# The second MoE's weight pieces: decoded in the y stages alone instead of in y and x2

## The chip, the cores and the metric

The kernel runs on one core of a Trainium2 chip. The metric is device time in microseconds of one execution, and the time before is the median of three runs, 1390.62 us (1390.1 to 1392.14). One execution was also taken by the hardware profiler; it took 1393.72 us, and its span from the first to the last instruction is 1391.8 us. The engines are named as the profile names them: PE (TensorE), DVE (VectorE), ACT (ScalarE), POOL (GpSimd), and SP, the engine whose queue issues nearly all transfers.

## What is computed

An attention block, a first MoE and a second MoE in a row; a token's vector has 512 numbers, and there are 8 x 576 = 4608 tokens.

```python
p_packed = sm_attn(p, k, v)              # 32 packed queries per head
out = sm_attn(q, p_packed, p_packed)     # softmax over 32
h = np.maximum(np.maximum(x @ w1, x @ w2), x @ w3)     # 512 -> 768
x2 = h @ w_out                                         # 768 -> 512
h = x2 @ w_in                                          # 512 -> 2048
g = P(h) / (Q(h) + 1e-06)                # polynomials of h, element by element
y = g @ w_out2                           # 2048 -> 512
```

The weights come in as 64-bit floats. The kernel decodes them itself, from two 32-bit words each, into a high and a low part in fp32, and each large product is made of three: high by high, high by low, low by high (`mm3`, lines 60 to 63).

## The kernel before, in words

The first 593 us of the span handle the batches in four pairs (`bp`, 0 to 3); the second MoE follows over blocks of 512 tokens. Each pair has two stages.

*y stage* (`y_stage`, line 447). For each of six column blocks f and both batches b2, three products (w1, w2, w3) go into PSUM tiles `psy`, of which there are two. ACT copies the first into `hm` (L459), and DVE takes the maximum with the second and third (L461). ACT then makes the high part `hh`, and POOL (DVE in pair 0) the low part `hl`. After each of the 36 products, counted t = 0 to 35, `between` (line 540) does small steps of other work: the m stage for the next f (`m_stage`, line 303, PE's line 313, at t mod 6 of 2 and 4), a step of the next pair's attention (the list PACK), and, at the t in `y_steps`, one step of the decode of the second MoE's weights.

*x2 stage* (`x2_stage`, line 468). Eight products (m of 4, b2 of 2) with `w_out`, each of 36 matmuls into `psy`; ACT or DVE copies it out (L477) and it is stored to DRAM. Between them stand the second half of the next pair's attention (the list SECOND: a softmax on POOL, DVE and ACT, lines 267 to 297, and the first two m stages of the next pair) and, for the indices in `windows`, more steps of the decode. Pair 3 has neither.

*The decode* (`decode`, line 68, called through `Feed`, line 103). There are 32 pieces of 128 x 512 weights. Each is loaded (512 KB, L100, three buffers `w_raw`), taken apart by DVE (L76, L80), converted by ACT (L81, L82), put together by DVE (L85, L87, L92) and POOL (L95) into a `wt` tile, and stored to DRAM (512 KB, L235), from where the second MoE loads it. `step()` is `finish()` of one piece and then `start()` of the next: L76, L80, L81 and L82 belong to the start, the others to the finish, and the load of a later piece follows it. 33 steps decode 32 pieces.

*The wt tiles.* There are four (line 184). The m stage's own weights use them too: they were decoded in pair 0 and are loaded again from DRAM in later pairs (`again`, line 213, L216), four m stages ahead.

*The order.* The code is not run in the order in which it is written. With `schedule_with_timeline_sim` (line 731) a scheduler simulates the engines when the kernel is built, and fills each engine's queue; of the instructions that are ready in its simulation it takes the one that was written first, and it hands out tile buffers in the same way. On the chip each queue is then run strictly in that order.

Of the kernel before, what the change touches and what calls it, by code (L numbers as in the profile page):

```python
# [33 lines left out]
def attn_moe_moe2_kernel(  # L34
# [16 lines left out]
    def split(hi, lo, src, hi_eng="act", lo_eng="dve"):  # L51

        if hi_eng == "act":
            act.copy(hi, src)  # L54
        else:
            nc.vector.tensor_copy(hi, src)
        e = dve if lo_eng == "dve" else pool
        e.tensor_tensor(out=lo, in0=src, in1=hi.bitcast(F32), op=ALU.subtract)  # L58
# [165 lines left out]
    def w2_pieces():  # L224

        for i in range(32):
            box = []

            def tiles(box=box):
                box.append(wt_tile())  # L230
                hi, lo = (box[0][:, x] for x in range(2))
                return (hi.bitcast(I32) if wide else hi.bitcast(F32R)), lo.bitcast(F32R)

            def keep(box=box, i=i):
                nc.sync.dma_start(w2_scr[:, :, 512 * i : 512 * i + 512], box[0])  # L235

            yield tiles, w_2[i], keep, False

    def load_w2(tiles, o, n):

        for x in range(2):
            nc.sync.dma_start(tiles[:, x].bitcast(F32), w2_scr[:, x, 512 * o : 512 * (o + n)])
# [56 lines left out]
    def m_tiles(f):  # L299

        return [mp[f % 2].tile([128, 2, 2, 384], F32R, name=f"m{x}") for x in "hl"]

    def m_stage(bp, g, mt):

        ps = ps_t.tile([128, 2, 512], F32, name="pst")
        wt, n = next_wt()
        for b2 in range(2):
            for h in range(4):  # L310
                i, j = divmod(h, 2)
                l, c = slice(64 * j, 64 * j + 64), 32 * (h ^ b2)
                pe.matmul(ps[c : c + 32, b2, :384], lhsT=ppk[l, bp % 2, 2 * g + b2, 32 * h : 32 * h + 32],  # L313
                          rhs=wt[l, 384 * i : 384 * i + 384], start=True, stop=True)
        again(n)
        split(*(t[:, :, g, :] for t in mt), ps[:, :, :384])
# [130 lines left out]
    def y_stage(b2, f, m, a2, between, lo_eng):  # L447
        hm = hx.tile([128, 2, 288], F32, name="hm")
        mh, ml = m
        for w in range(3):  # L450
            ps = ps_y.tile([128, 2, 512], F32, name="psy")
            for half in range(2):
                for g in range(2):
                    ah, al = a2[g]
                    c = slice(288 * half, 288 * half + 288)
                    mm3(ps[:, half, :288], mh[:, g, 128 * w : 128 * w + 128], ml[:, g, 128 * w : 128 * w + 128],
                        ah[:, c], al[:, c], g == 0, g == 1)
            if w == 0:
              act.copy(hm, ps[:, :, :288])  # L459
            else:  # L460
              dve.tensor_tensor(out=hm, in0=ps[:, :, :288], in1=hm, op=ALU.max)  # L461
            between()
        hh = hp_pool.tile([128, S], F32R, name=f"hh{b2}{f}")
        hl = hp_pool.tile([128, S], F32R, name=f"hl{b2}{f}")
        split(hh, hl, hm.rearrange("p a b -> p (a b)"), lo_eng=lo_eng)
        return hh, hl

    def x2_stage(b, m, hs):
        ps = ps_y.tile([128, 2, 512], F32, name="psy")
        for half in range(2):  # L470
            c = slice(288 * half, 288 * half + 288)
            for f in range(6):
                hh, hl = hs[f]
                mm3(ps[:, half, :288], wo_h[:, m, 128 * f : 128 * f + 128], wo_l[:, m, 128 * f : 128 * f + 128],
                    hh[:, c], hl[:, c], f == 0, f == 5)
        xs = hx.tile([128, 2, 288], F32, name="hm")
        (act.copy if m < 3 else dve.tensor_copy)(xs, ps[:, :, :288])  # L477
        nc.sync.dma_start(x2_scr[:, m, S * b : S * b + S], xs.rearrange("p a b -> p (a b)"))

    def wi_at(f):  # L480

        if f < 1:
            return wi_0
        return wi_b[:, :, f - 1]
# [26 lines left out]
    pool.memset(cln[:, 1:2], -LN64)  # L511
    feed2 = None

    y_steps = {1: range(1, 36, 4), 2: range(1, 36, 4), 3: range(1, 32, 4)}
    windows = (), (0, 2, 4, 6), (1, 3, 5)
    for bp in range(NBP):
        turn = itertools.count()
        if bp == 1:
            feed2 = Feed(wp, w2_pieces(), NRAW, NRAW)
        if bp == NBP - 1:  # L520

            nc.sync.dma_start(av, a_in.partition_broadcast(128))
            nc.sync.dma_start(bv, b_in.partition_broadcast(128))
            dve.tensor_scalar(out=babs, in0=bv, scalar1=-1.0, scalar2=None, op0=ALU.mult)
            dve.tensor_tensor(out=babs, in0=babs, in1=bv, op=ALU.max)
        now = ahead
        a2, mt = ahead.a2, ahead.mt
        hs = [[None] * 6, [None] * 6]
        if bp + 1 < NBP:
            ahead = Ahead(bp + 1)  # L530
            for x in "P L0 W0 L1 W1".split():
                ahead.do(x)
            pack = ahead.steps(PACK)
        else:
            pack = iter(())
        for f in range(6):
            if f < 5:
                nmt = m_tiles(f + 1)

            def between(bp=bp, f=f, now=now):  # L540
                t = next(turn)
                if now.soft:
                    now.do("g")
                if f < 5 and t % 6 in (2, 4):
                    m_stage(bp, t % 6 // 2 - 1, nmt)
                if t >= 2:
                    next(pack, None)
                if bp == 0:
                    if t % 3 < 2 and t < 32:
                        feed.half_step()  # L550
                elif t in y_steps[bp]:
                    feed2.step()

            if bp == NBP - 1 and f == 2:
                load_w2(wi_at(0), 0, 1)
            for b2 in range(2):
                hs[b2][f] = y_stage(b2, f, [t[:, b2] for t in mt], a2[b2], between,
                                    "dve" if bp == 0 or (b2, f) == (1, 5) else "pool")
            mt = nmt
        if bp + 1 < NBP:  # L560
            assert not list(pack)
            gen = ahead.steps(SECOND)
            for m in range(4):
                for b2 in range(2):
                    x2_stage(2 * bp + b2, m, hs[b2])
                    next(gen, None)
                    if bp == 0:
                        feed.half_step()
                    if 2 * m + b2 in windows[bp]:
                        feed2.step()  # L570
            if bp == 0:
                assert not feed.raw and not feed.half
            next(gen, None)
            assert not ahead.soft
        else:
            assert not feed2.raw and not feed2.half
            rstack.close()
            NQA = 1
            wr = ctx.enter_context(tc.tile_pool(name="wr", bufs=1, side="right"))
            xpa = ctx.enter_context(tc.tile_pool(name="xpa", bufs=1, side="right"))  # L580
            wi_b = wr.tile([128, 2, 15, 512], F32R, name="wi_b")
            wq_a = wr.tile([128, 2, NQA, DM], F32R, name="wq_a")

            def wq_at(f):
                return wq_a[:, :, f] if f < NQA else wq_b[:, :, f - NQA]

            def load_x(blk, xp):
                xh = xp.tile([128, 4, 512], F32R, name="xh")
                xl = xp.tile([128, 4, 512], F32R, name="xl")
                for kc in range(4):  # L590
                    xr = xp.tile([128, 512], F32, name="xr", bufs=1)
                    nc.sync.dma_start(xr, x2_scr[:, kc, 512 * blk : 512 * blk + 512])
                    split(xh[:, kc, :], xl[:, kc, :], xr, lo_eng="pool" if blk > 1 else "dve")
                return xh, xl

            loads = [(wi_at(f), f) for f in range(1, 16)] + [(wq_at(f), 16 + f) for f in range(NQA)]
            per = -(-len(loads) // 8)
            for b2 in range(2):
                for m in range(4):
                    for _ in range(min(per, len(loads))):  # L600
                        tiles, o = loads.pop(0)
                        load_w2(tiles, o, 1)
                    if (b2, m) == (0, 2):
                        xc = load_x(0, xpa)
                    x2_stage(2 * bp + b2, m, hs[b2])
# [129 lines left out]
```

## Time and profile before

| | |
|---|---|
| median of three runs | 1390.62 us |
| the profiled execution | 1393.72 us |
| its span | 1391.8 us |
| PE busy in the span | 1313.8 us (94%) |
| DVE, ACT, POOL busy | 76%, 58%, 17% |
| pair 0, y and x2 | 54.0 to 171.0 and to 215.8 us |
| pair 1, y and x2 | to 297.4 and to 350.4 us |
| pair 2, y and x2 | to 432.7 and to 487.5 us |
| pair 3, y and x2 | to 554.5 and to 593.0 us |

The busy shares are means over stages with different limits, so the stages are looked at one by one. The bounds of a stage are read from the names on PE's matmuls: psy<-a2h,mh is a product of y, psy<-hh,wo_h one of x2. A busy PE is not a PE at full speed, so the granted clock stands beside the busy time.

### The profile page before, as it was taken

What the parts mean: (1) busy time and instruction counts of PE and PEld (TensorE: products, weight loads), DVE (VectorE), ACT (ScalarE), POOL (GpSimd) and SP (SyncE); (2) the same over time, 40 slices, a digit from 0 to 9 for tenths busy, and PEclk for the clock granted to TensorE, in tenths of its full rate; (3) what the DMA queues carried; (4) which work ended last, traced back from release to release, by engine and by line L of the source; (5) the groups of instructions that cost most, each with busy time, mean ns of one, the idle gap of its engine ahead of it and who ended that gap; (6) DMA issues with size and microseconds to landing.
All of it is one profiled execution on the core that took longest, in us unless ns stands there. A gap on an engine that the chain in (4) does not pass through costs nothing.

```text
span 1391.8 us, 21572 instructions
## 1 busy us (share of the span) xinstructions
PE 1313.8 (94%) x8496; PEld 1091.5 (78%) x8496; DVE 1051.1 (76%) x1630; ACT 802.2 (58%) x1337; POOL 242.7 (17%) x230
## 2 busy tenths in 40 slices
PE   4479899998999899999999999999999999999998
PEld 1267788878878789978888888888888888888886
DVE  5877845767677765178888988888888888888887
ACT  3444523543443333176766867768677686776765
POOL 3542242425333533000100101001010010100000
PEclk9589899999999999999999999999999999999999
DMA  9945544677464721970100101001001010010000
GB/s 307 308 138 167 158 144 145 213 230 245 155 209 156 237 93 55 325 278 1 47 14 1 61 1 38 23 0 62 0 25 37 0 54 0 16 38 1 31 0 31
DMA packets 51557, 140.86 MB, mean 101 GB/s; under 512 B 5632, under 2 KB 5632, under 8 KB 50688
## 3 DMA queue, kind: packets, MB, share of 16 engines
q1 hardware_dynamic: 51168, 138.96, 30.0%
q8 instruction: 67, 1.10, 0.3%
q10 hardware_dynamic: 288, 0.52, 0.1%
q14 instruction: 34, 0.28, 0.1%
HBM read 99.09 MB, written 40.37 MB: 100 GB/s over the span
## 4 chain that ended last, share of the span: by engine, by line
PE 81%; DVE 5%; DMA 4%; ACT 2%; issue 1%; POOL 1%; SPq 0%; ACTq 0%; POOLq 0%; DVEq 0%
PE po L61 10%; PE po L62 9%; PE po L63 9%; PE psh L62 9%; PE psh L61 9%; PE psh L63 9%; PE psy L61 8%; PE psy L62 7%; PE psy L63 7%; PE pst L313 2%; DMA wi_b<-w_scr 1%; DMA w_raw<-in_w_dram 1%; DMA x_scr<-hm 1%; PE pst L378 1%; DVE wt L87 1%
## 5 line engine op out<-in xcount | busy, mean ns | idle before, releaser
L61 PE MATMUL po<-wq_b,gh 128*128 128x512 f32 x540 | 212.3, 393 | 0.8 <-ACT gh L54 0.8
L62 PE MATMUL po<-wq_b,gh 128*128 128x512 f32 x540 | 211.3, 391 | 0.0
L62 PE MATMUL psh<-xl,wi_b 128*128 128x512 f32 x540 | 211.0, 391 | 0.0
L63 PE MATMUL psh<-xh,wi_b 128*128 128x512 f32 x540 | 210.6, 390 | 0.0
L61 PE MATMUL psh<-xh,wi_b 128*128 128x512 f32 x540 | 210.6, 390 | 0.0
L634 ACT ACTIVATE hb<-psh,babs 128x512 f32<-128x512 f32 (+1 forms) x145 | 100.2, 691 | 188.8 <-PE psh L63 188.8
L61 PE MATMUL psy<-a2h,mh 128*128 128x288 f32 x576 | 181.6, 316 | 17.1 <-DVE hm L461 8.1
L63 PE MATMUL po<-wq_b,gl 128*128 128x512 f32 x540 | 181.7, 391 | 0.0
L637 DVE SCALAR_TENSOR_TENSOR hb<-h,babs,hb 128x512 f32<-128x512 f32 (+1 forms) x145 | 108.2, 746 | 97.1 <-ACT h L635 97.0
L62 PE MATMUL psy<-a2l,mh 128*128 128x288 f32 x576 | 172.7, 300 | 4.4 <-POOL a2l L58 4.4
L63 PE MATMUL psy<-a2h,ml 128*128 128x288 f32 x576 | 172.0, 299 | 0.0
L58 POOL TENSOR_TENSOR xl<-xr,xh 128x512 fp32r<-128x512 f32 x28 | 36.6, 1306 | 633.5 <-ACT xh L54 633.5
L61 PEld LDWEIGHTS psy<-a2h,mh 128*128 128x128 f32 x576 | 110.3, 192 | 44.4 <-issue 12.9
L61 PE MATMUL psy<-hh,wo_h 128*128 128x288 f32 x384 | 117.2, 305 | 12.1 <-ACT hm L477 11.7
L63 PEld LDWEIGHTS po<-wq_b,gl 128*128 128x128 f32 x540 | 101.3, 188 | 24.0
L461 DVE TENSOR_TENSOR hm<-psy,hm 128x576 f32<-128x576 f32 x96 | 72.4, 754 | 63.2 <-PE psy L63 60.3
L61 PEld LDWEIGHTS po<-wq_b,gh 128*128 128x128 f32 x540 | 101.4, 188 | 22.9 <-ACT gh L54 1.2
L62 PEld LDWEIGHTS po<-wq_b,gh 128*128 128x128 f32 x540 | 101.4, 188 | 22.4
L61 PEld LDWEIGHTS psh<-xh,wi_b 128*128 128x128 f32 x540 | 101.4, 188 | 22.1
L62 PEld LDWEIGHTS psh<-xl,wi_b 128*128 128x128 f32 x540 | 101.4, 188 | 21.7
L63 PEld LDWEIGHTS psh<-xh,wi_b 128*128 128x128 f32 x540 | 101.4, 188 | 21.7
L62 PE MATMUL psy<-hl,wo_h 128*128 128x288 f32 x384 | 115.5, 301 | 0.0
(104 smaller groups left out, 2816.0 us busy)
## 6 DMA issues: line engine op xcount, KB each, us to landing
w_raw<-in_w_dram SPq DMA_DIRECT2D x32, 512.0 KB, 4.7
w_scr<-wt SPq DMA_DIRECT2D x32, 512.0 KB, 3.3
wt<-w_scr SPq DMA_DIRECT2D x36, 384.0 KB, 4.0
kt<-in_k_dram SPq DMA_DIRECT2D x16, 576.0 KB, 6.2
vraw<-in_v_dram SPq DMA_DIRECT2D x16, 576.0 KB, 6.5
w_raw<-in_w_dram SPq DMA_DIRECT2D x12, 768.0 KB, 12.0
kt<-in_q_dram SPq DMA_DIRECT2D x16, 576.0 KB, 6.2
x_scr<-hm SPq DMA_DIRECT2D x32, 288.0 KB, 3.3
```

The source lines that it names most:

```text
L58: e.tensor_tensor(out=lo, in0=src, in1=hi.bitcast(F32), op=ALU.subtract)
L61: pe.matmul(out_ap, lhsT=lh, rhs=rh, start=first, stop=False)
L62: pe.matmul(out_ap, lhsT=lh, rhs=rl, start=False, stop=False)
L63: pe.matmul(out_ap, lhsT=ll, rhs=rh, start=False, stop=last)
L87: dve.scalar_tensor_tensor(out=hib, in0=hw, scalar=-0x80000000, in1=t, op0=ALU.bitwise_and, op1=ALU.bitwise_or)
L313: pe.matmul(ps[c : c + 32, b2, :384], lhsT=ppk[l, bp % 2, 2 * g + b2, 32 * h : 32 * h + 32], rhs=wt[l, 384 * i : 384 * i + 384], start=Tru ...
L378: pe.matmul(pv[32 * h : 32 * h + 32, :64], lhsT=at[:, 3 * i + cp, o : o + 32], rhs=vt[:, h, c, :], start=c == 0, stop=c == VC - 1)
L461: dve.tensor_tensor(out=hm, in0=ps[:, :, :288], in1=hm, op=ALU.max)
L634: act.activation(hb, h, AF.Abs, scale=babs[:, 0:1])
L637: dve.scalar_tensor_tensor(out=hb, in0=h2, scalar=babs[:, 1:2], in1=hb, op0=ALU.mult, op1=ALU.add)
```

## The change

The steps of the decode of the second MoE's pieces are taken out of x2, and there are more of them in y: after every third product in pairs 1 and 2 (12 each instead of 9), and after every fourth, with one more at the end, in pair 3 (9 instead of 8). The steps in x2, 4 in pair 1 and 3 in pair 2, go. The number of steps stays 33.

```diff
-    y_steps = {1: range(1, 36, 4), 2: range(1, 36, 4), 3: range(1, 32, 4)}
-    windows = (), (0, 2, 4, 6), (1, 3, 5)
+    y_steps = {1: range(1, 36, 3), 2: range(1, 36, 3), 3: range(1, 36, 4)}
...
                     next(gen, None)
                     if bp == 0:
                         feed.half_step()
-                    if 2 * m + b2 in windows[bp]:
-                        feed2.step()
```

## Rows read from the trace of the kernel before

**Rows 1.** Stages: start:end, length, then busy us (records) PE, PEld, DVE, ACT, POOL, clock.

```profile
54.00:171.00 117.00, 93.16 (x900) 74.02 (x908) 95.04 (x136) 56.74 (x92) 38.98 (x36) 0.85 0.53 172
171.00:215.80 44.80, 44.41 (x401) 40.03 (x386) 19.54 (x34) 11.74 (x18) 14.92 (x12) 1.00 0.38 126
215.80:297.40 81.60, 79.31 (x869) 66.68 (x876) 52.49 (x91) 37.24 (x69) 29.79 (x34) 1.00 0.60 188
297.40:350.40 53.00, 47.59 (x401) 43.14 (x388) 39.19 (x66) 19.60 (x31) 24.77 (x18) 0.94 0.74 253
...
432.70:487.50 54.80, 48.48 (x433) 43.08 (x433) 43.22 (x71) 21.39 (x33) 25.89 (x19) 0.94 0.71 235
487.50:554.50 67.00, 65.41 (x530) 58.96 (x530) 38.29 (x53) 24.58 (x38) 22.31 (x16) 1.00 0.21 72
```

**Rows 2.** What TensorE waited for, x2 of pairs 1 and 2: us, times, longest.

```profile
PE psy L61 <- ACT hm L477: 5.4, 3, 2.4
...
PE psy L61 <- ACT hm L477: 6.3, 2, 5.3
```

**Rows 3.** Timeline before one wait: start, duration us, instruction, [idle before, releaser].

```profile
310.00 1.54 POOL L283 TENSOR_TENSOR e<-e,mx 128x576 f32<-128x576 f32 x1 [1.94 <-DVE mx L282]
...
310.44 1.38 DVE L80 TENSOR_SCALAR dec_r<-w_raw 128x512 int32<-128x512 int32 x1
...
311.85 0.63 ACT L82 ACTIVATE dec_r<-dec_r 128x512 f32<-128x512 int32 x1 [1.95 <-DVE dec_r L80]
...
312.96 0.62 ACT L477 COPY hm<-psy 128x576 f32<-128x576 f32 x1
```

**Rows 4.** Two stretches behind waits, columns as above.

```profile
313.60:317.20 3.60, 3.57 (x15) 3.57 (x16) 3.60 (x9) 0.63 (x1) 2.17 (x2) 0.53 0.48 185
466.20:473.00 6.80, 6.80 (x35) 6.80 (x36) 6.50 (x12) 2.71 (x4) 5.28 (x4) 0.66 0.77 259
```

**Rows 5.** Line 87 in y1, its x2, pair 2's x2, y3: ns, starts.

```profile
L87 DVE SCALAR_TENSOR_TENSOR wt<-w_raw,dec_t x7: 681/692/932, 226.1 to 294.0; 128x512 int32<-128x512 int32 x7
...
L87 DVE SCALAR_TENSOR_TENSOR wt<-w_raw,dec_t x6: 681/1025/1404, 298.9 to 326.0; 128x512 int32<-128x512 int32 x6
...
L87 DVE SCALAR_TENSOR_TENSOR wt<-w_raw,dec_t x7: 650/687/1416, 434.3 to 473.4; 128x512 int32<-128x512 int32 x7
...
L87 DVE SCALAR_TENSOR_TENSOR wt<-w_raw,dec_t x5: 679/693/1206, 501.3 to 526.2; 128x512 int32<-128x512 int32 x5
```

**Rows 6.** Stages, tile w_raw alone: length, DVE, POOL (y0, y1, x2 of 1).

```profile
54.00:171.00 117.00, 46.26 (x49) 7.85 (x4) 0.85 0.53 172
215.80:297.40 81.60, 19.47 (x34) 9.65 (x7) 1.00 0.60 188
297.40:350.40 53.00, 23.27 (x32) 7.85 (x6) 0.94 0.74 253
```

**Rows 7.** Line 313 alone, x2 of pairs 1 and 2: length, PE.

```profile
297.40:350.40 53.00, 2.84 (x48) 0.83 (x34) 0.94 0.74 253
...
432.70:487.50 54.80, 5.24 (x80) 1.81 (x79) 0.94 0.71 235
```

**Rows 8.** Waits in y of pair 1, DVE's and SP's: us, times, longest.

```profile
DVE wt L87 <- PE pst L313: 1.8, 1, 1.8
...
SPq L216 <- DMA w_scr<-wt: 15.4, 6, 5.4
```

**Rows 9.** Stretches of y with three, no and three pieces, columns as first.

```profile
257.30:281.00 23.70, 22.93 (x255) 18.47 (x255) 18.71 (x32) 13.34 (x28) 10.92 (x14) 1.00 0.73 221
281.00:293.00 12.00, 12.00 (x130) 11.34 (x128) 4.25 (x6) 4.05 (x6) 2.86 (x3) 1.00 0.65 216
392.00:416.00 24.00, 22.51 (x252) 18.01 (x250) 19.70 (x32) 12.85 (x27) 10.66 (x14) 1.00 0.65 211
```

**Rows 10.** Timeline of SP's queue where the decode ends.

```profile
529.47 3.79 SPq L235 DMA_DIRECT2D w_scr<-wt  x2
554.63 6.47 SPq L242 DMA_DIRECT2D wi_b<-w_scr  x11
```

## The prediction

> **What bounds the kernel now.** I read the busy time by stage first, then the waits of TensorE in the stages that the change touches, then the instructions around the longest of these waits. The stages are named by pair of batches (0 to 3) and kind: y (the first MoE's three products) and x2 (its output product).
>
> The table by stage [rows 1] shows a kernel that TensorE (PE) bounds nearly everywhere: in y of pair 1 it is busy 79.31 of 81.60 us, in y of pair 3 65.41 of 67.00. The two exceptions that matter here are x2 of pairs 1 and 2: 47.59 of 53.00 and 48.48 of 54.80, with a granted clock of 0.94. Pair 0 has the same x2 with the same 401 matmul records as pair 1 and takes 44.80 us, at a clock of 1.00 and with VectorE (DVE) busy 19.54 instead of 39.19. So x2 of pair 1 is 8.2 us longer than it has to be. Pair 2 has 32 records more, of the m stage's product, whose time is 5.24 against 2.84 us [rows 7], so 2.4 us; 54.8 - 44.8 - 2.4 leaves 7.6 us too many. 15.8 us is what lies in these two stages.
>
> Where it is lost: PE waits there for nothing but ScalarE's (ACT's) copy of a finished x2 product out of PSUM, three times and 5.4 us in pair 1, twice and 6.3 us in pair 2, one of them of 5.3 us [rows 2]. The chain behind one [rows 3]: POOL runs a softmax subtraction of 1.54 us; beside it the decode's mask on DVE (L80) takes 1.38 us; ACT's conversion (L82) waits 1.95 us for that; and the PSUM copy (L477), which waited for nothing of the decode, stands behind L82 in ACT's queue and starts at 312.96. PE has waited 2.4 us when it ends. After such a wait the granted clock is lower: 0.53 over 3.6 us in pair 1 and 0.66 over 6.8 us in pair 2 [rows 4], so 1.7 and 2.3 us more, at half speed by the lower of the two levels (1.2 instead of 2.4 GHz) for part of these stretches. The waits and the slow stretches together make up about the 8.2 and 7.6.
>
> **The change, part by part.** It writes no instruction less: 33 calls of step() stand before and after, 32 pieces are decoded, each with its 512 KB load and its 512 KB store on SP's queue. What moves is the place. Written before: 9 calls in y of pair 1, 4 in its x2, 9 and 3 in pair 2, 8 in y of pair 3. After: 12, 0, 12, 0, 9. But the order on the chip is not the written one. Pieces finish on DVE (L87) 7 times in y of pair 1, 6 in its x2, 7 in x2 of pair 2, 5 in y of pair 3 [rows 5]; the other 7 of the 32 are in y of pair 2. Written, it would be 8, 4, 9, 3, 8 (the first call only starts a piece). The scheduler draws pieces of the next pair forward into x2, and one out of y lags into it.
>
> What lets it do so are the four wt buffers, which the pieces share with the reloaded weights of the m stage, and these are loaded four ahead. A piece gets a buffer when an m stage's product frees one (DVE stood 1.8 us before L87 for that), and a reload when a piece's store has landed (SP waited 15.4 us in six waits) [rows 8]. Buffers go by written order. So I went through that order with the change: two pieces, two reloads and again in y, and at its end pieces 8 to 10 behind the next pair's first m stage, whose product is the one that DVE waited 1.8 us for: there piece 6 is finished today, at 294.0 [rows 5, 8]. That gives 9 pieces in y of pair 1 and three (9, 10, 11) in its x2: the piece behind these is written at product 4 of the next y, behind two reloads that take the buffers. For pair 2 the same count gives 9 and 5, and 6 in y of pair 3. So x2 keeps 3 of 6 and 5 of 7: five pieces move, not seven.
>
> *x2 of pair 1.* Six pieces start between 298.9 and 326.0 [rows 5], 5.4 us apart. Three end at about 310, so the wait that ended at 313.6 stays and the two behind it go: 5.4 - 2.4 = 3.0 us, and one slow stretch of 1.7. That is 4.7 us. Bounds: 0, if the pieces that stay keep all waits, and 8.2.
>
> *x2 of pair 2.* Seven between 434.3 and 473.4, 6.5 apart; five end at about 460, just where the wait of 5.3 us begins today (it and its slow stretch are 7.6 us). It may stay or go; I take half, 3.8. Bounds 0 and 7.6.
>
> *The y stages.* Two pieces more in pairs 1 and 2, one more in pair 3. A piece costs DVE 19.47 / 7 = 2.8 us here, and 23.27 / 6 = 3.9 in x2 [rows 6], where the softmax keeps POOL busier beside it. The cover is there on average: DVE is busy 52.49 of 81.60 [rows 1]. It is thin in places. Where three pieces stand in 24.0 us (DVE 19.70) PE was idle 1.49 us, in another such stretch 0.77; without a piece, 0 of 12.0 [rows 9]. That is 0.3 to 0.5 us a piece. A fourth piece in the 23.7 us would bring DVE to 18.71 + 2.8 = 21.5, so I take a little more, 0.6 us for each of five: 3.0 us. Bounds 0 and 18.5 (the slower rival). What would be late is the maximum that empties psy (L461): PE has two of these buffers, and DVE takes its queue in order.
>
> *The end of the decode.* One piece more in y of pair 3, whose last store is issued within the 3.79 us from 529.47; the first load that waits for these weights' space is issued at 554.63 [rows 10]. 21 us of cover, so nothing. SP's queue carries the same transfers; a store waits at its head for POOL's product (L95), and the pack's loads stand behind it, but PE waited for no load in x2 [rows 2] and lost only 2.3 us in all in y, so nothing; if a kt or vraw load came late it would be about another 2 us, once.
>
> **Sum.** -4.7 - 3.8 + 3.0 = -5.5 us. On the profiled execution, 1393.72 us (span 1391.8, the rest around it), 1388.2. The median of the runs is 1390.62, 3.1 lower; I take the difference to that: 1385 us. Below 0.2% (2.8 us) a measurement of this kernel can't be told from no change.
>
> **Rivals.**
> 1. *x2 is freed altogether.* The pieces that stay stand in the first 12 us, ahead of the softmax's POOL work, and no copy is held up: -8.2 - 7.6, y absorbs all: 1374.8 us. For it: x2 of pair 0, where DVE has half the work, has hardly an idle PE. Against: the first wait of pair 1 has its cause within the pieces that stay.
> 2. *The price moves with the piece, or the scheduler draws the pieces back.* x2 costs 8.2 / 6 = 1.4 and 7.6 / 7 = 1.1 us a piece; taken off by count that is 3 x 1.4 + 2 x 1.1 = 6.4 us, and five pieces at 1.2 in y give 6 back: 1390 us. The same if x2 still holds six and seven. For it: POOL makes hl in y, and 1.4 us of a piece runs there too (9.65 / 7 [rows 6]). Against: the DVE time of a piece is 1.1 us lower in y. The Trainium skill, SBUF — State Buffer, section "Who interferes with whom", says that VectorE and GpSimd share a port pair as a lock, and whichever comes second waits until the other's instruction has ended; it names DVE operations with two SBUF inputs and copies and scalar operations in their two-port modes. The trace agrees that such collisions are there (the mask of 1.38 us beside POOL's 1.54 [rows 3]). By the rule alone a piece would pay the same lock in y and the time would be this rival's; the DVE time of a piece [rows 6] says that y has fewer collisions.
> 3. *Slower: DVE becomes the bound in y.* The price is in y of pair 0, where 46.26 us of decode on DVE go with 117.00 us [rows 1, 6]: 35.4 us more than pair 1 for 26.8 us more decode, so 1.3 us for each us, 3.7 for a piece, 18.5 for five. Less the 8.5 saved, +10: 1400.6 us. It decides from 8.5 / 5 = 1.7 us a piece. For it: 21.5 of 23.7 us in the stretch above, when DVE was busy only 95.04 of 117.00 in pair 0. Against: pair 0 also has its low part hl on DVE, waits for its first data and a clock of 0.85, and pair 1 with seven pieces lost just 2.3 us.
>
> **How the numbers follow.** Forecast 0.52, with a range of its own from 1380 to 1389; rival 1 0.14, rival 2 0.17, rival 3 0.17. The range leaves out the lower half of rival 1 (0.07) and most of rival 3 (0.12): 1375.5 to 1395. Faster: most of the forecast and all of rival 1, 0.62. Within 0.2%: rival 2 and the forecast's upper end, 0.21. Slower: rival 3, 0.17.
>
> **What would show it.** L87 in x2 of pairs 1 and 2: three and five (six and seven mean rival 2). The waits of PE for L477 at about one of 2.4 us in pair 1 and the 5.3 in pair 2 gone or not. The stages: x2 at about 48 and 51 us (44.8 and 47.2: rival 1), y of pairs 1 and 2 at 83 and 83.5 (over 85.5: rival 3, with PE waiting for DVE's L461). Wrong altogether would be a difference in y of pair 3's end, in the second MoE behind it, or a y that gets shorter.

## The result and the profile after

The changed kernel takes 1402.77 us, median of four runs (1399.78 to 1406.32); the kernel before, on the same chip, 1390.73 (1390.1 to 1392.14). The ratio is 1.0086, with a 95% interval from 1.0071 to 1.0101: 12 us slower, where 5.5 us faster was forecast, and above the range. The profiled execution took 1400.71 us, with a span of 1398.8.

For a table by stage both traces are cut at the first matmul of each stage, so that a stage holds the same matmul records in both (within two). Columns are those of [rows 1]: start:end, length, busy us (records) of PE, PEld, DVE, ACT and POOL, granted clock, DMA share, GB/s. The rows are y of pair 1, its x2, y of pair 2, its x2, y of pair 3. Before:

```profile
215.70:298.70 83.00, 80.71 (x893) 67.11 (x891) 53.76 (x93) 38.25 (x71) 29.79 (x34) 1.00 0.59 187
298.70:350.30 51.60, 46.19 (x377) 42.71 (x371) 37.92 (x64) 18.59 (x30) 24.77 (x18) 0.93 0.75 256
350.30:434.00 83.70, 80.71 (x892) 67.09 (x890) 54.81 (x93) 38.18 (x71) 29.51 (x34) 1.00 0.50 162
434.00:487.40 53.40, 47.08 (x409) 42.61 (x403) 41.95 (x69) 20.44 (x32) 25.89 (x19) 0.94 0.72 238
487.40:554.40 67.00, 65.41 (x530) 58.96 (x529) 38.29 (x53) 24.58 (x38) 22.31 (x16) 1.00 0.21 72
```

And after:

```profile
212.90:306.60 93.70, 83.92 (x893) 69.23 (x891) 62.14 (x103) 40.26 (x75) 31.62 (x36) 0.96 0.58 189
306.60:352.90 46.30, 43.16 (x378) 39.68 (x372) 26.23 (x49) 14.84 (x24) 18.77 (x15) 1.00 0.63 217
352.90:442.70 89.80, 82.56 (x893) 68.04 (x891) 64.16 (x103) 40.36 (x75) 31.69 (x36) 0.98 0.53 175
442.70:494.20 51.50, 45.84 (x409) 41.68 (x403) 32.90 (x59) 17.33 (x28) 22.27 (x17) 0.97 0.61 205
494.20:562.50 68.30, 65.75 (x531) 59.06 (x530) 42.11 (x58) 26.04 (x40) 23.62 (x17) 1.00 0.25 86
```

x2 became shorter, by 5.3 and 1.9 us. The y stages became longer, by 10.7, 6.1 and 1.3. Together that is +10.9 us. (This profiled span is only 7.0 longer than that of before, since it also starts its first y 2.7 us earlier and is 1.2 shorter elsewhere, both outside the change.) In y of pair 1 the idle time of PE, length less busy time, went from 2.3 to 9.8 us, and the same 893 matmuls took 3.2 us more: the clock is 0.96 instead of 1.00.

Where the pieces are finished (line 87, in the order of the table; answers to [rows 5]):

```profile
L87 DVE SCALAR_TENSOR_TENSOR wt<-w_raw,dec_t x9: 691/694/1881, 223.2 to 301.9; 128x512 int32<-128x512 int32 x9
...
L87 DVE SCALAR_TENSOR_TENSOR wt<-w_raw,dec_t x3: 671/679/694, 306.8 to 317.8; 128x512 int32<-128x512 int32 x3
...
L87 DVE SCALAR_TENSOR_TENSOR wt<-w_raw,dec_t x9: 682/694/1917, 363.5 to 438.0; 128x512 int32<-128x512 int32 x9
...
L87 DVE SCALAR_TENSOR_TENSOR wt<-w_raw,dec_t x5: 679/692/1285, 442.9 to 469.2; 128x512 int32<-128x512 int32 x5
...
L87 DVE SCALAR_TENSOR_TENSOR wt<-w_raw,dec_t x6: 678/694/1212, 508.1 to 537.3; 128x512 int32<-128x512 int32 x6
```

That is 9, 3, 9, 5 and 6, as counted in the prediction. The waits view after (us, times, longest): PE and DVE in y of pair 1, then DVE in y of pair 2, then PE in the two x2 (these two answer to [rows 2]).

```profile
PE psy L61 <- ACT hm L459: 5.1, 2, 3.9
PE psy L337 <- DVE hm L461: 1.8, 1, 1.8
...
DVE wt L87 <- DMA w_scr<-wt: 6.0, 4, 4.5
DVE wt L87 <- PE pst L313: 2.2, 2, 1.8
...
DVE wt L87 <- DMA w_scr<-wt: 1.9, 3, 0.9
...
PE psy L61 <- ACT hm L477: 3.0, 2, 2.4
...
PE psy L61 <- ACT hm L477: 5.6, 2, 5.1
```

The third line is new. Before, DVE's L87 waited in this stage only for an m stage's product, 1.8 us once [rows 8]. Now it waits four times until a piece's store to `w_scr` has landed: 6.0 us. And PE waits for L459, the copy that empties `psy`, which it did not do in y before. The timeline of after shows how the two hang together (start, duration us, instruction, [idle before, releaser]):

```profile
279.96 0.58 SPq L235 DMA_DIRECT2D w_scr<-wt  x1
...
286.91 0.69 DVE L87 SCALAR_TENSOR_TENSOR wt<-w_raw,dec_t 128x512 int32<-128x512 int32 x1 [4.45 <-DMA w_scr<-wt]
287.64 0.43 DVE L92 TENSOR_SCALAR w_raw<-wt 128x512 int32<-128x512 int32 x1
288.11 0.43 DVE L76 TENSOR_SCALAR dec_t<-w_raw 128x512 int32<-128x512 int32 x1
...
288.63 0.72 ACT L81 ACTIVATE dec_t<-dec_t,reb 128x512 int32<-128x512 int32 x1 [4.77 <-DVE dec_t L76]
289.26 0.62 ACT L459 COPY hm<-psy 128x576 f32<-128x576 f32 x1
...
289.93 0.61 PE L61 MATMUL psy<-a2h,mh 128*128 128x288 f32 x1 [3.94 <-ACT hm L459]
```

A store is issued at 279.96 and lands at 286.9. Until then DVE stands before L87, which overwrites the `wt` tile that the store reads. L92 of this piece and L76, the first mask of the next, stand behind it in DVE's queue; ACT's L81 waits for L76, and the PSUM copy L459, which needs nothing of the decode, stands behind L81 in ACT's queue. PE has waited 3.94 us when it ends. Behind the wait the clock is low:

```profile
285.00:289.90 4.90, 0.99 (x8) 0.71 (x6) 2.60 (x5) 1.25 (x2) 1.49 (x1) 0.98 0.56 222
289.90:293.50 3.60, 3.57 (x16) 3.57 (x17) 1.89 (x4) 1.31 (x2) 0.00 (x0) 0.55 0.73 237
```

At 0.55 PE is for most of these 3.6 us on the lower of its two levels (1.2 and 2.4 GHz). So this is the chain of [rows 3] again, in y, with a transfer at its head instead of a softmax. The kernel before issued a store at the same place, and it took about as long. There it held up a reload of the m stage's weights in SP's queue (the wait of L216 in [rows 8]), and no engine:

```profile
277.72 0.57 SPq L235 DMA_DIRECT2D w_scr<-wt  x1
...
284.71 0.80 SPq L216 DMA_DIRECT2D wt<-w_scr  x2
```

Why a piece meets a store now: with nine steps in y, pieces and reloads mostly alternate, and a piece takes a tile that an m stage's product sets free (of the seven L87 three start about 0.1 us behind the end of such a product, three come later and wait for nothing, and one waited 1.8 us for it). With twelve, two pieces come one after the other, and every second one takes the tile of the piece before. Its four waits end at 229.3, 248.6, 267.2 and 286.9, where the stores issued at 225.94, 244.69, 263.89 and 279.96 land.

The other waits for a store in y of pairs 1 and 2 are short, 0.25 to 0.87 us, but five of these six put L87 beside POOL's L58, which had begun up to 0.25 us before it. L87 then takes 1.73 to 1.92 us instead of 0.69, and the same chain follows, through the mask L76 to ACT and PE. One of the three of pair 2:

```profile
423.26 1.43 POOL L58 TENSOR_TENSOR hl<-hm,hh 128x576 fp32r<-128x576 f32 x1 [3.31 <-ACT hh L54]
423.32 1.91 DVE L87 SCALAR_TENSOR_TENSOR wt<-w_raw,dec_t 128x512 int32<-128x512 int32 x1 [0.85 <-DMA w_scr<-wt]
...
427.43 0.40 PE L61 MATMUL psy<-a2h,mh 128*128 128x288 f32 x1 [1.66 <-ACT hm L459]
```

Behind the five, PE waits 1.78 us (for L461, the second line of the waits view) and 1.11 us in pair 1, and 1.76, 1.15 and 1.66 us in pair 2. With the 3.94 us from above that is 6.8 us in y of pair 1, where PE's idle time grew by 7.5, and 4.6 us in y of pair 2, where it grew by 4.2. Behind the waits of 1.78 and 1.76 us the granted clock is low too, 0.72 over 3.7 us and 0.68 over 3.6 us. An estimate from these rows, the waits and of each slow stretch the part by which its clock lies under 1, gives 9.4 of the 10.7 us and 5.7 of the 6.1 us. Start less wait, each of the five L87 would have begun ahead of L58; that is read from the trace, and no run takes only the collision away.

A wait for a store also stands in the chain of the long wait in x2 of pair 2. The mask L76 is queued behind that L87, ACT's L81 waits for the mask, and the copy L477 stands behind L81:

```profile
463.16 0.69 DVE L87 SCALAR_TENSOR_TENSOR wt<-w_raw,dec_t 128x512 int32<-128x512 int32 x1 [1.89 <-DMA w_scr<-wt]
...
467.40 0.61 PE L61 MATMUL psy<-hh,wo_h 128*128 128x288 f32 x1 [5.12 <-ACT hm L477]
```

Before, no L87 waited for a store in that stage; ahead of its wait of 5.3 us, L87 and the mask L76 took 1.38 and 1.37 us beside POOL's work. So PE's wait there has its old size, but not its old chain.

### The profile page after: what moved, and what is told of

The parts are those of the page before. It is cut to its first block, busy times and chain, and to the rows that moved or that the text cites. A ratio compares the mean times of both kernels' runs of the same rounds, so it can differ in the third digit from the quotient of the medians.

```text
span 1398.8 us, 21569 instructions
## 1 busy us (share of the span) xinstructions
PE 1314.1 (94%) x8496; PEld 1090.7 (78%) x8496; DVE 1054.1 (75%) x1630; ACT 800.9 (57%) x1337; POOL 237.9 (17%) x230
## 4 chain that ended last, share of the span: by engine, by line
PE 71%; DMA 8%; DVE 7%; ACT 2%; issue 2%; POOL 2%; SPq 0%; POOLq 0%; ACTq 0%; DVEq 0%
PE po L61 9%; PE po L62 9%; PE po L63 9%; PE psh L62 9%; PE psh L61 9%; PE psh L63 9%; PE psy L61 5%; PE psy L63 4%; PE psy L62 4%; DMA w_raw<-in_w_dram 3%; DMA w_scr<-wt 2%; DVE wt L87 1%; POOL wt L95 1%; DMA wi_b<-w_scr 1%; DMA x_scr<-hm 1%
## 5 line engine op out<-in xcount | busy, mean ns | idle before, releaser
L61 PE MATMUL psy<-a2h,mh 128*128 128x288 f32 x576 | 183.2, 318 | 26.9 <-DVE hm L461 10.9
L58 POOL TENSOR_TENSOR xl<-xr,xh 128x512 fp32r<-128x512 f32 x28 | 36.5, 1304 | 632.5 <-ACT xh L54 632.5
L62 PEld LDWEIGHTS psy<-a2l,mh 128*128 128x128 f32 x576 | 112.1, 195 | 5.1 <-POOL a2l L58 5.1
L633 ACT ACTIVATE u<-psh,av 128x512 f32<-128x512 f32 (+1 forms) x145 | 113.9, 785 | 1.6 <-DVE gl L58 1.4
```

What stands on the lines that cost most here:

```text
L61: pe.matmul(out_ap, lhsT=lh, rhs=rh, start=first, stop=False)
L62: pe.matmul(out_ap, lhsT=lh, rhs=rl, start=False, stop=False)
L633: act.activation(u, h, AF.Identity, scale=av[:, 3:4], bias=av[:, 2:3])
```

## The experiments

Two theories. **A, the store:** the loss is DVE's wait for the store of the piece before, handed on to ACT and PE. **B, the amount:** DVE has too much to do in y, as in rival 3, and the waits only show it. All ratios are to the kernel before on the same chip, with 95% intervals. A kernel with an edit in `decode` has its lines moved by a few: L462 and L464 stand for L459 and L461, L95 for POOL's new copy.

**1. The store reads another tile** (`e1_const`), so that no `wt` tile waits for it. Left out: the decoded weights never reach the second MoE. The number and the size of the stores stay.

```diff
-                nc.sync.dma_start(w2_scr[:, :, 512 * i : 512 * i + 512], box[0])
+                nc.sync.dma_start(w2_scr[:, :, 512 * i : 512 * i + 512], wo_h.rearrange("p a b -> p (a b)")[:, :1024].rearrange("p (x n) -> p x n", x=2).bitcast(F32))
```

> The changed kernel, but each piece's 512 KB store takes its bytes from wo_h instead of from the piece's wt tile, so that a wt tile is free as soon as POOL has written it (left out: the second MoE's decoded weights never reach it). Decode, order of steps and traffic stay. Theory A (DVE's L87 stands at the head of its queue until the store of the piece before has landed, and ACT's and PE's work stands behind it): the wait for w_scr<-wt, 6.0 us in y of pair 1 and 1.9 in pair 2, is gone, y falls from 92 to 84-88 and from 88 to 83-86, in all 1388-1396 us. Theory B (two more pieces are simply too much work for DVE in y, with its collisions with POOL): nothing of that changes, y stays at 90-92 and 87-89, 1400-1404 us.

1405.66 us, 1.0099 [1.0065, 1.0133]: no gain in all. By stages: the waits for the store are gone, y of pairs 1 and 2 take 88.4 us each, with eleven pieces in each, at a clock of 1.00, and x2 46.2 and 48.5. But x2 of pair 0 went from 43.5 to 60.5, and there the chain is another one:

```profile
PE psy L275 <- ACT hm L477: 9.5, 1, 9.5
...
ACT hm L477 <- DMA x_scr<-hm: 11.1, 1, 11.1
```

The edit freed the stores from their pieces as well: four of them are issued at 186.17, in x2 of pair 0 and before any piece is finished, and a store of x2 issued at 192.92 lands after 8.5 us. In y of pairs 1 and 2 no L87 takes more than 0.69 us. The run speaks for A in the stages of the change, but it isn't a clean one.

**2. Before, with more DVE work** (`e2_dve`): the masks L76, L80 and L92 twice for steps in y of pairs 1 and 2.

```diff
-        dve.tensor_scalar(out=t, in0=hw, scalar1=keep, scalar2=None, op0=ALU.bitwise_and)
+        for _ in range(1 + twice[0]):
+            dve.tensor_scalar(out=t, in0=hw, scalar1=keep, scalar2=None, op0=ALU.bitwise_and)
```

> The kernel before, with the three masks of each piece that is decoded from y of pairs 1 and 2 (L76, L80, L92) issued twice: 3 x 0.43 us for 7 to 9 pieces, 9 to 11 us more of DVE in each y, about what the change adds there (27.6 - 19.5 = 8.1 us), and no piece, buffer or transfer more. Theory A: y has room for it, 82-85 us each, 1390-1396 us in all. Theory B: y of pairs 1 and 2 grow to 88-92 us like the changed kernel's, 1402-1412 us.

1407.18 us, 1.0113 [1.0089, 1.0138]: what B expects. y of pair 1 takes 93.3 us with DVE busy 68.22, and the wait for a store is 0.9 us, once. The scheduler also finished nine and eight pieces in y of pairs 1 and 2 instead of seven each, so that this isn't DVE's amount alone. More work on DVE can thus cost as much as the change did, with what it does to the order. That doesn't show that it is the change's cost; runs 5 and 11 have to say that.

**3 and 4. A reload for three m stages ahead instead of four**, in the kernel after (`e3_after_d3`) and before (`e4_before_d3`), to leave a tile more to the pieces.

```diff
-        n += NWT
+        n += NWT - 1
```

> The changed kernel with the m stage's weights loaded again three m stages ahead instead of four, so that one of the four wt tiles is free for pieces at any time. Theory A: L87 waits for a store no longer (under 1 us in each y), y of pair 1 at 83-86 and of pair 2 at 83-85, x2 stays at 46-47 and 50-52, in all 1383-1392 us. Theory B: 1398-1404 us.

> The kernel before with the m stage's weights loaded again three m stages ahead instead of four. Theory A: there DVE waited for a buffer only 1.8 us in y of pair 1 and 1.1 in its x2, so 1387-1392 us. If the free tile only lets the scheduler pack more pieces into x2 or y, and theory B holds, 1392-1400 us.

After: 1404.56 us, 1.0086 [1.0059, 1.0112], y at 92.3 and 93.7. Before: 1390.10, 0.9990 [0.9976, 1.0003]. The tile that came free did not end the wait in the kernel after: in y of pair 1 L87 still waits four times and 4.6 us for stores.

**5. Less DVE work in the changed kernel** (`e5_light`): two of the three masks of a piece are left out (lines 80 and 92).

```diff
-            dve.tensor_scalar(out=r, in0=hw, scalar1=0x1FF, scalar2=None, op0=ALU.bitwise_and)
...
-            w = hw
-            dve.tensor_scalar(out=w, in0=hib, scalar1=-0x00800000, scalar2=None, op0=ALU.bitwise_and)
+            w = hib
```

> The changed kernel with less work on DVE per piece: the masks L80 and L92 are left out (so the low parts of the second MoE's weights are wrong), ACT's L82 reads the raw word instead. About 1.9 instead of 3.0 us of DVE a piece, so 9 pieces cost about 17 us in y, less than the 19.5 of 7 pieces in the kernel before; buffers, stores, loads and steps stay. Theory A (the wait for a store at the head of DVE's queue, handed on to ACT and PE): these waits are still there, y of pair 1 stays over 88 us and of pair 2 over 86. Theory B (DVE's amount of work): y at 81-84 us in both, in all 1376-1386 us.

1396.74 us, 1.0046 [1.0031, 1.0061]. The window of y of pair 1, then its waits (lines one lower than after):

```profile
213.20:306.50 93.30, 83.28 (x890) 69.38 (x888) 53.87 (x86) 40.04 (x74) 32.33 (x36) 0.96 0.61 196
```

```profile
DVE wt L87 <- DMA w_scr<-wt: 6.7, 2, 6.3
...
DVE dec_t L76 <- DMA w_raw<-in_w_dram: 3.0, 1, 3.0
...
PE psy L61 <- DVE hm L460: 7.1, 3, 4.0
```

DVE is busy 53.87 us, as in the kernel before (53.76), with ten pieces. The stage takes 93.3 all the same, and the store's wait is there; a wait of the next piece's mask for its raw words, 3.0 us, holds PE up a second time. B falls as the main cause of the loss in pair 1. In pair 2 the stage fell by just 1.7 us, to 88.1. In all the run is 6.0 us faster than the changed kernel, so DVE's amount isn't without a price.

**6. Reloads two ahead** (`e6_after_d2`): the edit of run 3 with `NWT - 2`.

> The changed kernel with the m stage's weights loaded again two m stages ahead instead of four, so that two wt tiles are free for pieces; with three ahead DVE still waited 4.3 us for stores in y of pair 1. DVE's work is the same. Theory A: L87's waits for stores under 1 us in each y, which fall to 84-88 us, in all 1386-1395 us. Theory B: y stays at 90-94 us, 1400-1405 us.

1412.46 us, 1.0164 [1.0147, 1.0181], with ten pieces in each of the two y. A miss: the wait for stores was still 5.1 us in four. The scheduler fills tiles that come free with pieces that it draws forward, so that one piece still follows another. Freeing a buffer is no way to take this wait away.

**7. The change in pair 1 alone** (`e7_pair1`).

```diff
-    y_steps = {1: range(1, 36, 3), 2: range(1, 36, 3), 3: range(1, 36, 4)}
+    y_steps = {1: range(1, 36, 3), 2: range(1, 36, 4), 3: range(1, 36, 4)}
+    windows = (), (), (1, 3, 5)
```

> The change in pair 1 alone (12 steps in its y, none in its x2); pair 2 keeps 9 and 3, pair 3 takes 9. If the cost stands in each pair by itself: y of pair 1 at 91-94 and its x2 at 46-48 us as in the changed kernel, pair 2 as in the kernel before (82-84 and 52-54), in all 1395-1398 us, about half of the change. If it needs both pairs, 1389-1393 us.

1399.94 us, 1.0064 [1.0049, 1.0079]. The loss stands in the pair that is changed: y of pair 1 at 94.2 (wait for stores 6.8 us in four, PE for L459 5.8), y of pair 2 at 84.0 and its x2 at 53.4, as before.

**8. Fewer steps in x2, put into pair 3** (`e8_mix`): y of pairs 1 and 2 as before, every third product in pair 3.

```diff
-    y_steps = {1: range(1, 36, 4), 2: range(1, 36, 4), 3: range(1, 32, 4)}
-    windows = (), (0, 2, 4, 6), (1, 3, 5)
+    y_steps = {1: range(1, 36, 4), 2: range(1, 36, 4), 3: range(1, 36, 3)}
+    windows = (), (0, 2, 4), ()
```

> Another place for the steps: 9 in y of pairs 1 and 2 as before, 3 in x2 of pair 1, none in x2 of pair 2, and 12 in y of pair 3, where DVE is busy only 38 of 67 us because there is no next pair to prepare. Both theories: y of pairs 1 and 2 stay at 82-84 us (seven or eight pieces each), x2 of pair 2 falls to 48-51, y of pair 3 grows to 68-70; in all 1383-1389 us.

1394.79 us, 1.0028 [1.0019, 1.0038], a miss: y of pair 3 went from 67.0 to 72.3 with nine pieces, PE waiting 5.0 us for L461 there, and x2 of pair 2 gained only 1.2.

**9 and 10. The wait moved to another queue**: L87 writes into DVE's own `dec_t`, and POOL copies this to the `wt` tile, so that POOL and not DVE stands before the store. In the kernel after (`e9_after_pool`) and before (`e10_before_pool`).

```diff
-        hib = hi if hi is not None and hi.dtype == I32 else t
+        late = hi is not None and hi.dtype == I32
+        hib = t
...
-            if hib is t:
+            if late:
+                pool.tensor_copy(hi.bitcast(F32), t.bitcast(F32))
+            else:
```

> The changed kernel, in which DVE's L87 writes the high part in place in dec_t (two tiles of its own) and POOL copies it into the wt tile ahead of L95, so that the wait for a store stands in POOL's queue and no longer in DVE's. DVE has the same work, POOL one copy more a piece. Theory A (the wait for the store at the head of DVE's queue is the cost): L87 waits for no store, y of pair 1 falls from 92-94 to 84-87 and of pair 2 from 88-90 to 84-87, x2 stays at 46-52, in all 1384-1393 us. Rival (pieces in y cost by their collisions with POOL, which has more to do here): y stays at 89-95, 1398-1410 us.

> The same edit in the kernel before: L87 in place, POOL copies the high part into the wt tile. There DVE waited only 1.8 us for a buffer in y of pair 1 and 1.1 in its x2. Theory A: little to gain, 1384-1392 us. Rival (collisions with POOL): one more POOL copy beside DVE's work makes y and x2 longer, 1393-1400 us.

After: 1390.75 us, 1.0015 [0.9997, 1.0034], 12.0 us less than the changed kernel. Before: 1394.43, 1.0030 [1.0018, 1.0042], 4 us more than without the edit. In all the copy is no gain in itself, but the changed kernel with it is no longer the slower one. By stages run 9 takes 2.8 and 3.1 us off y of pairs 1 and 2, and 1.8 and 6.3 us off their x2, where the wait of 5.1 us had a store in its chain as well. In run 10 y is 5.5 and 7.1 us longer than before and x2 3.1 and 5.4 shorter. (In both runs part of it is an m stage's product that moved from x2 into y.) The waits of run 9 in y of pair 1 (PE, DVE, POOL):

```profile
PE psy L61 <- DVE hm L464: 4.3, 3, 3.2
...
DVE dec_t L76 <- DMA w_raw<-in_w_dram: 4.6, 2, 3.7
...
POOL wt L95 <- DMA w_scr<-wt: 7.0, 3, 3.5
```

The stores are waited for as long as ever, 7.0 us, but by POOL, and PE doesn't notice. In the stretch of the worst wait another one took its place: the next piece's first mask stands 3.7 us for its raw words, whose load comes late behind the attention's loads, and L464 stands behind it.

**11. The same, and a fourth buffer for raw words** (`e11_pool_raw4`; `vraw` gives up one of two).

```diff
-    NRAW = 3
+    NRAW = 4
...
-        t = kp.tile([96, 4, VC, D], F32, name="vraw", bufs=2)
+        t = kp.tile([96, 4, VC, D], F32, name="vraw", bufs=1)
```

> The changed kernel with POOL's copy of the high part, and a fourth w_raw buffer (its space from vraw, of which one is left instead of two). What is left there in y of pair 1 is DVE's L76 at the head of the queue waiting 3.7 us for a piece's load, and PE 3.2 us behind it. Theory A, for any transfer at the head of DVE's queue: L76 waits under 1 us, y of pair 1 falls from 91 to 85-88 us, in all 1383-1389 us. Rival (the rest is DVE's and POOL's work): y of pair 1 stays at 89-92, 1388-1393 us.

1385.28 us (1384.33 to 1389.27), 0.9955 [0.9942, 0.9969]: faster than both kernels, by 5.6 and 17.5 us. The stages as in the tables above, without y of pair 3, then PE's waits in y of pair 1 for the maximum that empties `psy`:

```profile
216.50:303.10 86.60, 83.94 (x910) 67.88 (x909) 65.45 (x106) 41.41 (x76) 40.75 (x48) 1.00 0.71 222
303.10:347.00 43.90, 41.88 (x352) 39.08 (x353) 25.72 (x46) 13.92 (x22) 18.59 (x15) 1.00 0.55 194
347.00:433.60 86.60, 84.11 (x911) 67.80 (x909) 65.35 (x107) 41.49 (x77) 41.28 (x48) 1.00 0.64 206
433.60:479.40 45.80, 43.68 (x385) 40.00 (x385) 34.61 (x55) 16.21 (x26) 22.89 (x19) 1.00 0.56 196
```

```profile
PE psy L61 <- DVE hm L464: 1.1, 2, 0.9
```

DVE does more in y of pair 1 than in the changed kernel (65.45 against 62.14 us, ten pieces against nine), and yet the stage is 7.1 us shorter: this also speaks against B. No x2 has a slow clock any more. (Some 20 matmul records, an m stage's product, moved from each x2 into y, so y and x2 are best taken together: 130.5 and 132.4 us against 134.6 and 137.1 before.)

**12. Fewer pieces in pairs 1 and 2, more in pair 3** (`e12_late3`; run 11 with steps 9, 9 and 15).

```diff
-    y_steps = {1: range(1, 36, 3), 2: range(1, 36, 3), 3: range(1, 36, 4)}
+    y_steps = {1: range(1, 36, 4), 2: range(1, 36, 4), 3: range(1, 31, 2)}
```

> The same with the steps elsewhere: 9 in y of pairs 1 and 2, none in x2, 15 in y of pair 3 (every second product), where nothing of a next pair is prepared. Theory A: y of pairs 1 and 2 at 83-87 us, x2 at 45-50, y of pair 3 at 68-74, in all 1380-1389 us. Rival (DVE's and POOL's work decides): y of pair 3 grows to 75-80 us and eats the gain, 1389-1396 us.

1396.01 us, 1.0033 [1.0021, 1.0045], a miss. y of pair 3 went to 70.5 with ten pieces, and y of pairs 1 and 2 became longer than in run 11, 89.4 and 88.8, although they hold two pieces fewer each.

**13 and 14. Which of the two edits, and the edits without the change.** Open after run 11 was how much the raw buffer did alone (`e13_after_raw4`, the changed kernel with the last diff only) and what is left without the change (`e14_before_pool_raw4`, the kernel before with both edits).

> The kernel after with a fourth buffer for the raw words of the weights, and nothing else. Theory (in the change's pieces DVE stands at the head of its queue until the store of the piece before has landed, and that is most of the loss): the fourth raw buffer doesn't touch this wait, so the waits of the second write to wt for w_scr in y of pairs 1 and 2 stay at 3 to 8 us in all, y of pair 1 stays at 90 to 94 us; y of pair 0 falls from 118 to about 111; in all 1393 to 1398 us. Rival (the masks' wait for the raw words' load is what costs, not the store): y of pair 1 falls to about 86, and with y of pair 0 the whole is at 1383 to 1388 us.

> The kernel before with the same two edits as the best run so far (the high part goes to wt by POOL, a fourth raw buffer). It shows what the change's own placement of the pieces is worth once neither DVE wait stands. Theory: y of pair 0 at about 111 as there, y of pairs 1 and 2 at 83 to 85, x2 at 48 to 50: 1385 to 1390 us, so that the change's placement is worth 0 to 5 us by itself. Rival (the change's placement is worth nothing, the edits are all of the gain): 1381 to 1385 us, no slower than the kernel with the change and the edits.

Run 13: 1401.64 us, 1.0068 [1.0045, 1.0092], hardly less than the changed kernel. The store's wait is there as before, and so is PE's:

```profile
DVE wt L87 <- DMA w_scr<-wt: 7.7, 4, 4.4
...
PE psy L61 <- ACT hm L459: 5.1, 3, 3.7
```

y of pair 0 was expected to be shorter and is, 109.5 against 118.0 us, but it also starts 11 us later, and x2 of pair 0 starts 2.8 us later than in the changed kernel. The total of 1393 to 1398 us was missed for that. So what the raw buffer does alone can't be told from nothing: the interval overlaps that of the changed kernel. Its use comes only once the store's wait has left DVE's queue.

Run 14: 1397.65 us, 1.0051 [1.0036, 1.0065]. With the same edits the change itself makes it 12.4 us faster (run 11), where 0 to 5 were expected. Not all of it is the x2 stages. In this run, as in 10 and 12, y of pair 1 has a wait of an m stage's product for the low part of the one before:

```profile
PE pst L316 <- DVE ml L58: 2.3, 1, 2.3
```

It occurs once there and once in y of pair 2 in all three, which have steps at every fourth product and POOL's copy, and neither in run 9 nor in run 11, which have the copy and steps at every third. Why the scheduler's order comes out like that wasn't followed further.

## Why the prediction was wrong

**Right: what bounds x2, and what moves.** The placement was counted to the piece, 9, 3, 9, 5 and 6. x2 of pair 1 gave 5.3 us where 4.7 were forecast; its three waits of 5.4 us became two of 3.0, where one of 2.4 was to be left, and the clock went from 0.93 to 1.00. That the longer one is again 2.4 is luck: in it ACT's L477 stands behind the softmax's exponential, which waits for POOL, and not behind the decode's L82 as in [rows 3]:

```profile
326.60 0.68 ACT L285 ACTIVATE e<-e 128x576 f32<-128x576 f32 x1 [3.12 <-POOL e L283]
```

x2 of pair 2 gave 1.9 where 3.8 was taken as half of two cases. A long wait stands there (5.1 us after 5.3), but not the one of either case: its chain has a wait for a store in it, 1.89 us. Together 7.2 of the forecast 8.5. The end of the decode and what follows cost nothing (-1.0 us from the last x2 on).

**Wrong: the term of y.** It was 3.0 us, 0.6 a piece for five pieces, and measured 18.1, which is 3.6 a piece and nearly the upper bound of 18.5. The step that failed is "A piece gets a buffer when an m stage's product frees one", while only a reload was to wait until "a piece's store has landed" [rows 8]. In y that was true of the order before, not of the new one. The prediction went through the turns of the four tiles to count pieces, found "two pieces, two reloads and again", and did not ask what the second of two pieces waits for. It is the store of the first. The price of a piece was then taken from stretches in which no piece met a store [rows 9], so it held neither the wait nor the L87 that the wait puts beside POOL. With the wait off DVE's queue, the price of a piece was nearer to the forecast: in run 11 y of pairs 1 and 2 are 3.6 and 2.9 us longer than before for three pieces more each, 1.2 and 1.0 a piece, and part of this is the m product that moved; in run 1, without a store's wait, 5.4 for four, 1.4, with the same product in it.

**The sentence on SP's queue** was wrong as well: it asked whether PE waits for a load, and cost the stores and the pack's loads at nothing (no row stands behind its 2 us for a late load). Beside them the longest wait got its size. The store at the worst place stood behind the loads of `kt` and `vraw`, 576 KB each, issued at 277.24 and 278.42. The windows before and in its transfer (DMA share and GB/s are last), and the summary of the nine stores of that stage (L235):

```profile
244.70:248.70 4.00, 4.00 (x42) 3.20 (x41) 2.72 (x5) 2.88 (x6) 1.44 (x1) 1.00 0.73 227
...
280.00:287.00 7.00, 5.99 (x56) 4.92 (x54) 2.52 (x5) 2.00 (x3) 1.43 (x1) 1.00 0.99 338
```

```profile
DMA to landing us min/median/max: 3.3/3.4/6.9
```

The first window is that of a store which landed after 3.9 us, and DVE waited 0.3 for it; in the second the transfer engines are full and the store takes 6.9. The raw words of run 9 are late at the same place. This is shown by the coincidence in the traces; no run took the pack's loads away.

**The rivals.** Rival 3 had the sign and the size (+10 us), by the price of pair 0, but its mechanism, DVE's amount, isn't the main one: run 5 brought DVE's work in y of pair 1 back to that of before and left the stage at 93.3, and run 11 has more of it at 86.6. Run 2 shows that the amount can cost where it comes without slack, so the prediction was right to list it. Its sign, PE waiting for L461, came for 2.8 us in y of pair 1, against 5.1 for ACT's L459. Rival 1's stages, x2 of 44.8 and 47.2, came near in run 11 (43.9 and 45.8, with two and four pieces, and without the product that moved). Rival 2 stated that a piece costs in y what it costs in x2, and run 11's 1.0 to 1.2 is indeed near the 1.1 to 1.4 that it took. The collisions with POOL that it expected in y did come with the change, in five of the 18 L87 of pairs 1 and 2, each behind a wait for a store.

**What is shown and what not.** Shown: the new wait and its chains to PE, which account for most of the loss in y of both pairs (trace of after); that the wait stays when DVE's work goes (run 5), and that the loss stands in the changed pair alone (run 7). Moving the wait to a queue on which PE doesn't depend gives 12.0 us back in the changed kernel (run 9) and none in the kernel before (run 10). That edit changes the order as well, and its gain lies in x2 as much as in y, so the 12.0 us is not the price of the wait in y alone. Run 9 brought y of pair 2 from 89.8 to 86.7, so half of that loss goes with the edit. Not shown: how the loss divides between the time waited, the collisions that follow it and DVE's greater amount; no run changes one of them and leaves the order as it was.

## What to carry to other kernels

When a change shifts who shares a ring of buffers, go through the ring once more and write down for each turn not only when it comes, but whose release it waits for and on which engine's queue it waits. Here a release by a transfer cost nothing on the queue that issues transfers, and held up PE at the head of the queue of an engine that others wait for to empty PSUM. There one transfer beside other loads (6.9 us, where the median was 3.4) made the longest wait, and waits under 1 us cost more than they lasted, by what the shifted instruction ran into. And price an edit from a stretch that has the order it will have, or take the bound that includes the wait.

## What the runs showed of the hardware

- The time from issue to landing of the same 512 KB store ranged from 3.3 to 6.9 us within one stage, and the slowest stood where the DMA share was 0.99. The Trainium skill, DMA: Bandwidth & Descriptors, section "Anatomy of one DMA — SWDGE (gpsimd) path", fits a transfer's time (on another issue path) as a fixed 2.0 us and the bytes at 436 GB/s, which gives an estimate of 3.2 us here. The median of 3.4 us agrees with it; the 6.9 is what a transfer in company takes, and the trace decides there.
- The same L87 that takes 0.69 us took 1.91 beside POOL (at 423.32, shown in the section on the result). POOL's instruction began 0.06 us earlier, and L87 ended 0.54 us after it. A wait that shifts an instruction can thus put it beside another that it didn't meet: without its wait of 0.85 us and at 0.69 us, this L87 would have ended before POOL's began.
- A fourth buffer of raw words (with one fewer for `vraw`) made y of pair 0 7 to 9 us shorter, but it started 9 to 12 us later (in run 13 at 62.7 us, after 51.3 with the change alone). What delays the start wasn't looked into.
